# A linear-attention and feed-forward kernel: another written order of its steps, and GpSimd steps that wait for VectorE steps ahead of them

## The chip, the cores and the metric

The kernel runs on one core of a Trainium2 chip. A core has TensorE (PE, matrix products), VectorE (DVE), ScalarE (ACT), GpSimd (POOL) and SyncE (SP, which here issues all DMAs). Each engine works through its own queue in order; the queues are tied together by semaphores. The metric is the device time of one execution, in microseconds (us). A change is called faster or slower when it moves this time by more than 2%.

## The reference

Two parts follow each other. The first is a gated linear attention over 4 batches, 8 heads, 768 positions and a head width of 48; the second is a feed-forward part over the 3072 rows of 384 that come out.

```python
state = zeros((B, H, D, D))
for t in range(S):
    state = alpha[:, :, t, :, None] * state + einsum('bhd,bhe->bhde', k[:, :, t], v[:, :, t])
    y[:, :, t] = einsum('bhd,bhde->bhe', q[:, :, t], state)
x = y.transpose(0, 2, 1, 3).reshape(B * S, H * D)
h1 = x @ w1                      # 3072x384 @ 384x1024
h2 = x @ w2
out = maximum(h1, h2) @ w_out    # 1024x384
```

All inputs and the output are float32.

## The kernel before

**Tiling.** The 3072 positions are cut into twelve chunks of 256 (n = 0 to 11; three to a batch). A chunk needs four loads of 384 KB, alpha, k, q and v. For chunks 0 and 1 alpha is loaded in two halves, and many of the steps on them are cut in two as well, so `ka1.0` is the first half of step `ka` of chunk 1.

**A chunk's steps** (name, engine where it can go, line): `ln` the logarithm of alpha (ACT, L588); `su` the sum over pairs of positions (DVE or POOL, L596); `cs` the running sum by a triangular matrix (PE, L605 and L610); `inv`, `en`, `ep`, `gg` exponentials of it (ACT, L619 to L649); `ka` and `qi` products in place on k and q (DVE or POOL, L624, L629); `kt` and `qt` the scaled k and q in float16 (L661, L666); `vc` the cast of v (L488, L490 or L492, by engine); `tk` and `tq` their transposes (PE, L692), `ck` and `cq` the copies of these out of PSUM; from chunk 8 on DMA transposes `dk` and `dq` take the place of these four. `kv` makes the chunk's state terms (PE, L752); `t32`, `w` and `T` (L799, L810/L812, L787) carry the state on; `sc` the scores (PE, L832), `pt` their masked copy (DVE, L840); `yf` and `y` the output (PE, L877), and `xe` the cast of it into `xT` (ACT or DVE).

**The feed-forward part** uses max(h1, h2) = relu(x (w1 - w2)) + x w2. So `wd` forms w1 - w2 (L523), `wtp`/`wtc` transpose w2 (L507), `woc` casts w_out, and `mp`/`mc` form w2 times w_out (L532) once. The six weight loads are halves of w2, w_out and w1 (768 KB each; `ldw20`, `ldwo1` and so on, L467 and L470). Rows are worked in twelve groups of 256: `h` (PE, L943; `h0.4` is the product for the fifth and sixth of eight blocks of group 0), `r` the relu (L951 or L953), `o` the output product (PE, L976; parts a and b for each 128 rows), `ev` its copy out of PSUM, `st` the store. `h0.0` and `h0.2` need `wd0.0` and `wd0.1`; `h0.4` and `h0.6` need `wd1.0` and `wd1.1`.

**Fillers.** `fill` steps (L419) are products of a zero tile that nothing reads. They keep TensorE busy while it would wait in the opening.

**What sets the order.** Every step is declared to a planner with its dependencies, its possible engines and figures for its time (`plan.add`). The planner can search an order by itself, but where the text `ORDER` is not empty, `Plan.run` calls `Plan.follow` instead, which takes from that text the order of all steps, the engine of each (P, D, A, G, S) and the PSUM bank. The figures for time are then not read. The last loop of the kernel (L1007) emits the steps in that order. Dependencies between instructions on different engines become semaphore waits by what they read and write. `port=True` marks steps that the planner keeps from lying on VectorE and GpSimd at one time when it searches an order; before the change nothing in the emitted program enforces this.

SP's queue starts: `lda0.0 lda0.1 ldw21 lda1.0 ldk0.0 ldq0.0 lda1.1 ldw20 ldv0.0 ldwo0 ldw10 ldwo1 ldw11 ldq1.0 ldk1.0 ldv1.0`, then chunk 2.

Of the kernel before, what the change touches and what calls it, by code (L numbers as in the profile page):

```python
# [51 lines left out]
o0.1b:P inv2.0:A en2.0:A kt2.0:D y1:P xe3:D inv3.0:A ep2.0:A cs3.0:P5 tk2.0:P2 ev0.1:D xe2:A h1.0:P4 h1.2:P7 qi2.0:G qi3.0:G gg3.0:A en3.0:A ep3.0:A
r1.0:A h1.6:P1 ck2.0:D ka3.0:D kt3.0:G h1.4:P4 qt2.0:D r1.2:A gg2.0:A g2:G T4.1:G qt3.0:D vc2.0:A tq2.0:P o1.1a:P0 r1.4:A ldq4.0:S lda5.0:S r1.6:A
tk3.0:P6 ck3.0:A ln4.0:A inv4.0:A vc3.0:A kv2:P4 cq2.0:D sc2.0:P2 t32.4:G w4:D T4.0:G tq3.0:P T5.1:G pt2.0:D o1.1b:P o1.0a:P1 cq3.0:D ev1.1:D T5.0:G
yf2:P2 sc2.1:P4 pt2.1:D ldv4.0:S lda7.0:S sc3.1:P6 pt3.1:D su4.0:G cs4.0:P0 gg4.0:A en4.0:A ep4.0:A o1.0b:P ev1.0:A y2:P xe4:D xe5:A ka4.0:G qi4.0:G
qt4.0:D kt4.0:G ln5.0:A inv5.0:A kv3:P4 w6:D T7.0:G g4:G t32.7:G T7.1:G sc3.0:P6 pt3.0:D h2.0:P1 r2.0:A tk4.0:P2 ck4.0:A w7:D ldk5.0:S ldq5.0:S
h2.6:P0 tq4.0:P h2.4:P1 h2.2:P7 ldv5.0:S r2.6:D y3:P4 r2.2:D t32.8:G su5.0:D T8.0:D vc4.0:A kv4:P6 w8:D xe6:D cq4.0:A sc4.0:P2 r2.4:A xe7:A o2.0a:P0
t32.9:G qi5.0:G T9.1:G ln7.0:A inv7.0:A h3.0:P1 pt4.0:D o2.0b:P st0.0:S ev2.0:D lda6.0:S cs5.0:P5 gg5.0:A su7.0:D w9:D T8.1:G r3.0:A ka5.0:G en5.0:A
ln6.0:A ep5.0:A h3.2:P4 r3.2:D T9.0:D h3.6:P0 ldq6.0:S ldv6.0:S r3.6:A o2.1a:P1 h3.4:P4 r3.4:D ldk6.0:S yf4:P2 sc4.1:P6 pt4.1:D o2.1b:P ev2.1:A
qt5.0:D ldq7.0:S ldk7.0:S su6.0:G cs6.0:P4 gg6.0:A g5:G vc6.0:A en6.0:A ep6.0:A kt5.0:G ldv7.0:S lda8.0:S lda9.0:S o3.1a:P0 o3.0a:P1 cs7.0:P5 y4:P  # L60
ka6.0:D kt6.0:D kv6:P6 xe9:D w12:D T10.0:G inv6.0:A qi6.0:G t32.13:D w13:D o3.1b:P o3.0b:P ev3.1:D t32.10:G xe8:A ka7.0:G T10.1:G en7.0:A ep7.0:A
vc5.0:A gg7.0:A ev3.0:A h4.0:P3 tk5.0:P6 ck5.0:D r4.0:A qt6.0:D h4.2:P2 tq5.0:P cq5.0:D r4.2:A tk6.0:P0 ck6.0:A ldk8.0:S h4.4:P3 r4.4:A qi7.0:G
st0.1:S qt7.0:D ldk9.0:S lda10.0:S st1.1:S ldq9.0:S ldq8.0:S st1.0:S vc7.0:A tq6.0:P ln8.0:A cq6.0:A h4.6:P4 kv5:P6 sc5.0:P2 w10:D r4.6:D kt7.0:G
# [12 lines left out]
pt10.1:D st4.1:S st5.0:S o9.0a:P1 o9.1a:P0 vc11.0:A kv11:P6 t32.22:D w22:D T23.1:D T23.0:G y10:P xe20:A xe21:D sc11.0:P6 o9.1b:P ev9.1:A h10.0:P5
# [223 lines left out]
def kernel(  # L300
# [706 lines left out]
    for o in plan.run():  # L1007
        o.emit(o.eng)
# [31 lines left out]
```

## Time and profile before

| | us |
|---|---|
| median of 3 runs | 141.82 (141.81 to 143.49) |
| profiled execution | 141.61 |
| its span, first to last instruction | 139.8 |
| TensorE busy | 131.8 |
| VectorE busy | 100.2 |
| ScalarE busy | 80.5 |
| GpSimd busy | 67.7 |
| 41 fillers on TensorE | 13.3 |

HBM is read at 23.59 MB and written at 4.72 MB. The profile gives each engine's busy time in the span. Busy TensorE time contains fillers, and matrix products overlap the load of the next weights, so the time from the start of one step to the start of the next says more than the length of one instruction. Landing times of loads are read from the trace's DMA records: a load is in when the last of its sixteen pieces is. A line number, such as L943, is that of the kernel before.

### The profile page before, as it was taken

How to read it: one execution, taken by the hardware profiler on the slowest of the kernel's cores; microseconds unless marked ns; L12 is line 12 of the kernel's file. 1: busy time of each engine (PE TensorE's matmuls, PEld its weight loads, DVE VectorE, ACT ScalarE, POOL GpSimd, SP SyncE). 2: the span in 40 equal slices, each digit the busy share in tenths (PEclk: the TensorE clock that was granted, in tenths of full speed). 3: DMA queues.
4: the chain of work that ended last, by engine and by line, in shares of the span. 5: the costliest groups of instructions: out<-in, count | busy, mean ns of one | idle time of the engine just before them, and what ended most of it. 6: DMA issues, size and time to landing. Idle time of an engine off the chain costs nothing.

```text
span 139.8 us, 5453 instructions
## 1 busy us (share of the span) xinstructions
PE 131.8 (94%) x2346; PEld 93.7 (67%) x2346; DVE 100.2 (72%) x164; ACT 80.5 (58%) x163; POOL 67.7 (48%) x109
## 2 busy tenths in 40 slices
PE   6959996998999999999999999999999999999991
PEld 2336664754787687767886776777758866776770
DVE  7618657689997897797888959579876668583600
ACT  3337683677689599556897665674415552243041
POOL 6904390046858963885949996803850070300000
PEclk9999999999999999999999999999999999999999
DMA  4899999899999999999999999919904996545033
GB/s 110 268 277 329 355 382 333 201 251 267 266 253 266 262 267 282 248 232 235 274 272 266 312 279 122 250 26 208 288 24 77 187 202 182 177 155 188 4 109 113
DMA packets 64680, 30.76 MB, mean 220 GB/s; under 512 B 58896, under 2 KB 63120, under 8 KB 64656
## 3 DMA queue, kind: packets, MB, share of 16 engines
q1 hardware_dynamic: 64656, 30.41, 87.2%
q8 instruction: 18, 0.29, 0.9%
q14 instruction: 6, 0.05, 0.1%
HBM read 23.59 MB, written 4.72 MB: 202 GB/s over the span
## 4 chain that ended last, share of the span: by engine, by line
PE 73%; SPq 10%; DMA 9%; DVE 4%; issue 1%; ACT 1%; DVEq 0%
PE PS L976 31%; PE PS L943 21%; PE PS L877 9%; DMA ldf<-in_k_dram 9%; SPq L448 6%; PE PS L692 4%; PE PS L832 4%; SPq L467 3%; SPq L470 2%; PE PS L752 2%; PE PS L605 1%; DVE qk L490 1%; DVE w L812 1%; DVE ldf L629 0%; PE PS L419 0%
## 5 line engine op out<-in xcount | busy, mean ns | idle before, releaser
L976 PE MATMUL PS<-wo,g 128*128 128x384 f16 (+1 forms) x200 | 37.7, 320 | 0.0
L943 PE MATMUL PS<-xT,wd 128*128 128x256 f16 x288 | 35.9, 273 | 0.3 <-ACT xT L488 0.2
L840 DVE TENSOR_TENSOR pt<-PS,mask 128x1024 f16<-128x1024 f32 x24 | 28.9, 1218 | 6.1 <-PE PS L832 4.5
L943 PEld LDWEIGHTS <-wd 128*128 128x128 f16 x288 | 27.3, 98 | 5.4 <-DVE xT L490 0.6
L953 ACT ACTIVATE g<-PS 128x512 f16<-128x512 f32 x32 | 18.8, 598 | 13.0 <-PE PS L943 12.7
L976 PEld LDWEIGHTS <-g 128*128 128x128 f16 x200 | 18.6, 98 | 10.8
L488 ACT CAST xT<-PS 128x384 f16<-128x384 f32 x14 | 8.0, 592 | 17.2 <-PE PS L877 17.0
L787 POOL TENSOR_TENSOR T<-w,gg 48x192 f16<-48x192 f32 x17 | 9.4, 553 | 16.1 <-DVE w L812 9.8
L629 POOL TENSOR_TENSOR ldf<-ldf,inv 128x384 f32<-128x384 f32 (+1 forms) x10 | 9.8, 983 | 15.2 <-DMA ldf<-in_q_dram 13.3
L661 POOL TENSOR_TENSOR qkt<-ldf,en 128x768 f16<-128x768 f32 (+1 forms) x7 | 11.9, 1698 | 10.7 <-DVE ldf L624 8.5
L976 PE MATMUL PS<-m,xT 128*128 128x384 f16 (+1 forms) x75 | 15.8, 320 | 0.0
L419 PE MATMUL PS<-fz 128*128 128x512 f16 x41 | 13.3, 451 | 1.2 <-DVE fz L416 1.2
L588 ACT ACTIVATE loga<-ldf 128x768 f16<-128x768 f32 (+1 forms) x14 | 10.6, 754 | 5.7 <-DMA ldf<-in_alpha_dram 5.4
L951 DVE TENSOR_SCALAR g<-PS 128x512 f16<-128x512 f32 x16 | 10.9, 686 | 3.3 <-PE PS L943 3.2
L666 DVE TENSOR_TENSOR qkt<-ldf,PS 128x768 f16<-128x768 f32 (+1 forms) x14 | 11.6, 834 | 2.4 <-ACT PS L644 2.2
L692 PE MATMUL PS<-ident,qkt 128*128 128x128 f16 x128 | 10.3, 219 | 1.0 <-DVE qk L490 0.5
L488 ACT COPY outs<-PS 128x384 f32<-128x384 f32 (+1 forms) x15 | 6.8, 457 | 7.3 <-PE PS L976 6.4
L692 PEld LDWEIGHTS <-qkt 128*128 128x128 f16 x128 | 8.2, 97 | 3.5 <-issue 1.0
L877 PE MATMUL PS<-pt,v 64*64 64x128 f16 x576 | 10.2, 218 | 0.0
L596 POOL TENSOR_TENSOR s<-loga 128x384 f16<-128x384 f16 (+1 forms) x10 | 7.9, 799 | 4.4 <-ACT loga L588 4.2
L488 ACT COPY qk<-PS 128x1024 f16<-128x1024 f16 (+1 forms) x11 | 9.0, 820 | 1.8 <-PE PS L692 1.6
L488 ACT CAST v<-ldf 128x768 f16<-128x768 f32 (+1 forms) x11 | 8.1, 742 | 3.0 <-DMA ldf<-in_v_dram 3.0
(79 smaller groups left out, 199.3 us busy)
## 6 DMA issues: line engine op xcount, KB each, us to landing
ldf<-in_k_dram SPq DMA_DIRECT2D x12, 384.0 KB, 6.5
ldf<-in_q_dram SPq DMA_DIRECT2D x12, 384.0 KB, 5.8
ldf<-in_v_dram SPq DMA_DIRECT2D x12, 384.0 KB, 6.6
out_dram<-outs SPq DMA_DIRECT2D x23, 192.0 KB, 3.8
ldf<-in_alpha_dram SPq DMA_DIRECT2D x10, 384.0 KB, 5.8
ldf<-in_moe_w_dram SPq DMA_DIRECT2D x4, 768.0 KB, 8.1
ldf<-in_moe_w_out_dram SPq DMA_DIRECT2D x2, 768.0 KB, 9.8
ldf<-in_alpha_dram SPq DMA_DIRECT2D x4, 192.0 KB, 4.7
```

Source lines behind the costliest of these rows:

```text
L419: plan.add(f"fill{i}", {"PE": 0.21}, lambda eng: nc.tensor.matmul(bank(fb), lhsT=fz[:, 0:128], rhs=fz, start=True, stop=True, skip_group_c ...
L488: nc.scalar.copy(out=out, in_=in_)
L588: nc.scalar.activation(out=A["loga", n][:, hd].rearrange("p h j d -> p (h j d)"), in_=A["ld", n, "a"][:, hd].rearrange("p h d -> p (h d)") ...
L661: e.tensor_mul(out=hjd(qkts[i3], 1)[:, hd], in0=A["ld", n, "k"][:, hd].rearrange("p h (j d) -> p h j d", j=2), in1=f.unsqueeze(2).to_broad ...
L666: nc.vector.tensor_mul(out=hjd(qkts[i3], 0)[:, hd], in0=A["ld", n, "q"][:, hd].rearrange("p h (j d) -> p h j d", j=2), in1=f.unsqueeze(2). ...
L692: nc.tensor.transpose(t[:, a, r, j, :], src[:, j, r, :], ident16)
L840: nc.vector.tensor_mul(out=t.rearrange("p u r c -> p (u r) c"), in0=A["sc", n, hf].rearrange("p u (r c) -> p (u r) c", r=2), in1=mask.rear ...
L877: nc.tensor.matmul(dst, lhsT=lhsT, rhs=rhs, start=(x, u) not in begun, stop=done and ends[x, u] == i, skip_group_check=True)
L943: nc.tensor.matmul(t[:, i], lhsT=wd16[:, s, (f + i) * 128 : (f + i + 1) * 128], rhs=xT[:, s, a0 : a0 + W], start=(s == 0), stop=(s == 2), ...
L951: nc.vector.tensor_relu(o, i)
L953: nc.scalar.activation(out=o, in_=i, func=ACTF.Relu)
L976: nc.tensor.matmul(A["op", t0, c], lhsT=lhsT, rhs=rhs, start=(part == 0 and j == 0), stop=(part == 1 and j + 1 == len(todo[1])))
```

## The change

Three things are changed.

The text `ORDER` is replaced by another. It holds the same steps, with 43 fillers in place of 41. Both the order on each engine and the engine of some 100 steps differ. Among them: `pads0` goes to GpSimd, ahead of `setp1`; of `su`, `t32`, `qi`, `T`, `kt`, `ka` and `vc` 28 go from GpSimd to VectorE and 20 the other way; seven `vc` go from ScalarE to GpSimd. SP's queue now starts `lda0.0 ldw21 lda0.1 ldk0.0 ldq0.0 ldv0.0 ldw20 lda1.0 lda1.1 ldwo0 ldw10 ldwo1 ldw11 ldk1.0 ldq1.0 ldv1.0`. The order on the engines around chunk 1 and the first group:

```diff
 VectorE
-wd0.0 wd0.1 woc1.1 r0.0 wd1.0 wd1.1 qi1.1 ka1.0 kt1.0 ka1.1 qt1.1 ck1.0 qi1.0 qt1.0 w2 T3.1 cq1.0 su2.0 w3 pt1.0 pt1.1 kt2.0 xe3
+wd0.0 woc1.1 wd0.1 ka1.0 kt1.0 wd1.0 wd1.1 qi1.0 qt1.0 vc1.0 ck1.0 qt1.1 cq1.0 su2.0 w2 t32.3 ck1.1 w3 pt1.0 pt1.1 su3.0 kt2.0 xe2
 GpSimd
-T2.0 T2.1 kt1.1 t32.2 t32.3 T3.0 ka2.0 su3.0 qi2.0 qi3.0
+T2.1 T2.0 T1.1 t32.2 ka1.1 qi1.1 kt1.1 T3.1 T3.0 ka2.0 qi3.0 qi2.0
 TensorE
-mp0.1 mp0.2 mp0.0 fill h0.0 mp1.1 mp1.2 mp1.0 h0.2 h0.4 h0.6 o0.0a tk1.0 o0.0b kv1 tk1.1 tq1.0 fill tq1.1 fill fill fill sc1.0 o0.1a yf1 sc1.1 cs2.0 o0.1b y1
+mp0.0 mp0.2 mp0.1 h0.0 fill fill mp1.0 mp1.1 mp1.2 h0.2 tk1.0 h0.4 h0.6 o0.0a tq1.0 o0.0b kv1 tk1.1 fill tq1.1 sc1.0 o0.1a cs2.0 yf1 sc1.1 o0.1b y1
```

Some of the planner's figures are changed:

```diff
-xfer=(1.56 if n < 8 else 1.7) * (h1 - h0) / 8, lag=0.3 if n < 2 else 0.1))
+xfer=(1.535 if n < 8 else 1.63) * (h1 - h0) / 8, lag=0.5 if n == 1 and i else 0.35 if n < 3 else 0.15))
...
-    WX = {"w1": 786 / 370, "w2": 786 / 370, "wo": 2.12}
+    WX = {"w1": 2.12, "w2": 2.5, "wo": 2.12}
...
-xfer=WX[name], lag=1.3), buf)
+xfer=WX[name], lag={"w2": 2.0, "wo": 2.2, "w1": 2.8}[name]), buf)
...
-tr = plan.add(f"wtp{i}.{s}", {"PE": 0.74}, emit, ...
+tr = plan.add(f"wtp{i}.{s}", {"PE": 0.66}, emit, ...
```

And the loop that emits the steps makes the first instruction of a GpSimd step wait for the last VectorE step marked `port` that stands ahead of it in the order, unless an earlier GpSimd step already did. There are 25 such waits.

```diff
+    traced = nc.cur_bb.bb.instructions
+    ahead = None
     for o in plan.run():
+        n = len(traced)
         o.emit(o.eng)
+        if o.eng == "DVE" and o.port:
+            ahead = traced[-1]
+        elif o.eng == "POOL" and ahead is not None:
+            tc.add_manual_dep(traced[n], ahead.name,
+                              mybir.DependencyInfo(mybir.DependencyClass.Sync, mybir.DependencyReason.DATA), reason="port")
+            ahead = None
```

## The prediction

> **What bounds the kernel now.** I read the page first, then TensorE's busy time by stretches, then TensorE's and VectorE's timelines where the stretches show a loss, and last the pairs of VectorE and GpSimd instructions that lie beside each other. Part 1 of the page, two rows, and the engine row of the chain that ended last:
>
> ```profile
> PE 131.8 (94%) x2346; PEld 93.7 (67%) x2346; DVE 100.2 (72%) x164; ACT 80.5 (58%) x163; POOL 67.7 (48%) x109
> ...
> PE 73%; SPq 10%; DMA 9%; DVE 4%; issue 1%; ACT 1%; DVEq 0%
> ```
>
> TensorE is the engine that sets the end, but not from the start. The stretches (length, then busy time and instructions of PE, PEld, DVE, ACT, POOL, then granted clock, DMA share, GB/s) show where:
>
> ```profile
> 14.00:24.40 10.40, 9.26 (x168) 6.10 (x165) 6.69 (x10) 6.70 (x16) 4.49 (x9) 1.00 1.10 358
> 24.40:33.70 9.30, 8.55 (x97) 5.38 (x96) 7.62 (x15) 6.41 (x12) 3.38 (x5) 1.00 0.99 236
> 33.70:65.00 31.30, 31.11 (x640) 23.19 (x639) 27.43 (x40) 23.80 (x47) 21.57 (x30) 1.00 1.13 258
> 65.00:100.00 35.00, 34.87 (x750) 26.26 (x746) 27.87 (x43) 22.69 (x44) 23.95 (x31) 1.00 0.97 227
> 100.00:136.00 36.00, 35.87 (x637) 26.46 (x635) 22.46 (x34) 13.51 (x26) 7.11 (x11) 1.00 0.55 139
> ```
>
> From 33.7 to 136 us TensorE is idle 0.19 + 0.13 + 0.13 = 0.45 us: nothing that another engine does there can give much. What remains is the opening, where the chain runs over the loads, one of them the longest single piece (start, length):
>
> ```profile
> 15.57 12.70 DMA ldf<-in_k_dram
> ```
>
> That is chunk 1's k: landed at 28.27. TensorE's timeline from 24.4 us (start, length, line, operands, count, idle before and releaser):
>
> ```profile
> 24.42 2.11 PE L532 MATMUL PS<-wo,w2T 128*128 128x384 f16 x12 [1.07 <-ACT wo L488]
> 26.36 2.13 PE L943 MATMUL PS<-xT,wd 128*128 128x256 f16 x18
> 28.33 0.81 PE L976 MATMUL PS<-wo,g 128*128 128x384 f16 x4
> ...
> 31.85 0.38 PE L419 MATMUL PS<-fz 128*128 128x512 f16 x1
> 32.72 0.38 PE L692 MATMUL PS<-ident,qkt 128*128 128x128 f16 x4 [0.49 <-DVE qk L490]
> 32.94 0.81 PE L419 MATMUL PS<-fz 128*128 128x512 f16 x3
> 33.68 0.42 PE L832 MATMUL PS<-qk 48*64 48x128 f16 x16
> ```
>
> Starts from one step to the next give what a step costs: an `h` 0.66, `o…a` of an early group 0.65, `tk`/`tq` of a half chunk 0.22, a filler 0.21. Against that, this stretch loses 0.33 (after `o0.0a`, 0.98 long), 0.24 (after `tk1.1`), 0.87 (filler and wait before `tq1.1`) and three fillers, 0.65: 2.1 us. After 33.7 the same comparison finds about 1.2 us in all: 0.30 after `sc3.0`, 0.27 after `cs9.0`, 0.28 after `cs11.0`, the rest in pieces of 0.1. So 3.3 us is all that an order can win behind 24.4 us. Ahead of 24.42 it can win little: `mp1` needs `wo` half 1, which landed at 23.51, and its cast (0.83, to 24.37).
>
> **The figures in the plan (landing delays, transfer times, 0.66 for a transpose step).** They are read only where no order is written out; one is. Cost nothing.
>
> **The opening loads on SP's queue.** Same sixteen transfers in another order. Every prefix ends alike: through `wo` half 1 both orders hold the same twelve, so 23.5, and through `w1` half 1 the same thirteen (25.67). Chunk 0's v comes about 3.6 us earlier, chunk 1's alpha later (15.2 and 15.95 for its halves; they were 8.72 and 12.20), k of chunk 1 one place earlier (14th, where q landed at 26.89). Does alpha's delay reach `mp1`? ln1.0 15.75, su1.0 on GpSimd 16.35, t32.1 16.9, w1 on VectorE 17.35, T1.0 17.7, then pt0.1 and pt0.0 at 1.22 each: 20.15; y0 20.2 to 21.3 (before: 19.21 to 20.35), the xT cast and wd0.0 to 22.95, three `mp0` and `h0.0` to 23.95, two fillers to 24.4. It just fits: 0, without reserve. The setup moves on GpSimd (pads0 ahead of setp1, 1.3 us) delay the mask and su0.0 to about 6.7, where fourteen fillers of 0.43 cover it; the two fillers more (43 for 41) stand where TensorE waits for loads anyway: 0.
>
> **Chunk 1 on VectorE.** Before (start, length, idle before):
>
> ```profile
> 23.53 0.56 DVE L490 CAST wo<-ldf 128x768 f16<-128x768 f32 x1 [0.28 <-DMA ldf<-in_moe_w_out_dram]
> 24.01 0.68 DVE L951 TENSOR_SCALAR g<-PS 128x512 f16<-128x512 f32 x1
> 25.69 1.83 DVE L523 TENSOR_TENSOR wd<-ldf 128x768 f16<-128x768 f32 x2 [1.00 <-DMA ldf<-in_moe_w_dram]
> 27.44 0.35 DVE L629 TENSOR_TENSOR ldf<-ldf,inv 128x192 f32<-128x192 f32 x1
> 28.30 0.36 DVE L624 TENSOR_TENSOR ldf<-ldf 128x192 f32<-128x192 f32 x1 [0.51 <-DMA ldf<-in_k_dram]
> ```
>
> The wd pair begins the moment `w1` lands. In the new order ka1.0 and kt1.0 (0.36 + 0.56), which need k, stand ahead of wd1.0 and wd1.1 (0.95 each), which `h0.4` and `h0.6` need. k is queued behind `w1`, so VectorE now stands still for k with a ready wd behind it. With k at 26.89: ka1.0 27.3, kt1.0 27.9, wd1.0 28.85, wd1.1 29.75, qi1.0 30.1, qt1.0 30.65, vc1.0 31.0, ck1.0 31.4, qt1.1 31.95, cq1.0 32.4. TensorE: h0.2 to 27.03, tk1.0 28.2, h0.4 29.55, h0.6 30.45, o0.0a 31.1, tq1.0 31.35, o0.0b 32.5, kv1 32.85, tk1.1, one filler, tq1.1, and `sc1.0` at 33.55; before it was 33.68. Three fillers and their waits are gone, and about 2 us of new waiting before h0.4 has replaced them. When does k land? In the trace one of the sixteen pieces of `w1` half 0 landed 1.35 us behind the other fifteen (21.41 against 20.06), a 16 KB instruction fetch of 1.11 us lying on the DMA at 18.69, and that ring stays late down to q. Without it the 14th load is in at 25.66. Ends 25.66 and 26.89; I take the middle, 26.3, since a fetch hits some ring in either order, but not at a fixed place in it. `sc1.0` follows k: 32.95, so -0.7. Of this about 0.3 is given back: su3.0 (0.37, moved from GpSimd) now stands between pt1.1 and kt2.0 on VectorE, which has no idle from 34.4 to 37.7, and tk2.0 waits for kt2.0. Net -0.4; from the ends +0.1 and -1.1.
>
> **GpSimd's 25 waits.** A GpSimd step waits for the last of VectorE's steps marked as port users ahead of it in the order; all behind it in GpSimd's queue wait too. What it removes is seen here, first VectorE, then GpSimd:
>
> ```profile
> 58.16 1.09 DVE L596 TENSOR_TENSOR s<-loga 128x384 f16<-128x384 f16 x1
> ```
> ```profile
> 58.03 1.00 POOL L624 TENSOR_TENSOR ldf<-ldf 128x384 f32<-128x384 f32 x1
> ```
>
> A sum of 0.35 lasts 1.09 beside a GpSimd product. Added up over VectorE's su, t32, T and qi against the shortest of each form: 1.9 + 1.3 + 0.9 + 0.4 = 4.5 us, on GpSimd some 2.6. The Trainium skill ("SBUF — State Buffer", section "SBUF: two separate sides") says that the shared port pair is an exclusive lock and that the loser blocks for the whole instruction. That speaks against the wait: the hardware already lines the two up, so a semaphore can only choose who goes first, and for a copy with one input in SBUF (vc0.1, woc0.0, vc1.0, vc8.0: 4 of the 25 waits) outside the two-port modes it buys nothing. Taking the 4.5 us as won would give 137.1; by the lock rule it is a swap, gain 0. Mine is the trace's: TensorE idles 0.45 us after 33.7, so of the 4.5 only qi1.0's 0.38 at 30.24 lay on its path (inside the 2.1 above). The upper bound: ka1.1 now waits for qi1.0 (30.1), so qi1.1 and kt1.1 behind it end at 32.3 instead of 30.75, which kv1 needs; o0.0b covers that to 32.5. If h0.4 came without its wait the cover would go, and up to 1 us of it would show. I take 0, bounds -0.4 and +1.
>
> **Moved steps and SP's later queue.** With each moved step at its row's mean VectorE gets 0.8 us more, GpSimd loses 2.8, ACT 3: no bound changes. Chunk 3's v goes behind three loads of chunk 4: 46.3 instead of 42.04; its cast (0.82) is due before kv3 at 48.9, slack 1.8. Group 0's first store moves behind chunk 7's loads, landing about 67.4 instead of 56.2; the eighth output buffer is wanted at about 67.8: 0.4 to spare, then it would hold only a PSUM bank. Mode changes on TensorE: 54 in either order. pt5.1, which before ended 0.26 before y5, comes with some 9.95 us of VectorE work behind pt4.1 where 14.2 passed: slack instead. I count 0.7 of the 1.2 us of small losses as closed, bounds 0 and 1.1.
>
> **Sum and rivals.** The profiled execution took 141.61, 1.81 above its span of 139.8 and 0.2 below the median of 141.82. 141.6 - 0.4 - 0.7 = 140.5, and 0.1 for half of the distance to the median: 140.6.
> - Forecast, 140.6 (140.1 to 141.1), chance 0.50.
> - Swap: k at 26.89, the new wait for k eats the gap, and the late losses come back elsewhere: 141.5, chance 0.25. For it: k was 12.7 us under way. Against: fillers went.
> - All closed: k at 25.66, -1.1, and late losses -1.1: 139.4, chance 0.17. Against it: VectorE at 82% in that stretch and no slack at `mp1`.
> - Slower: VectorE's queue head. If k lands as late as before, 28.28, because a fetch hits its ring too, wd1.0 starts at 29.3, h0.4 at 30.3, and sc1.0 comes at 35.0: +1.3, 142.9, chance 0.08. It decides from a landing of about 27.0 on, one for one.
> - That the change does nothing of what it says: the figures do nothing; the lock already orders the engines. It then reduces to the swap.
>
> The range 139.2 to 142.2 leaves out most of the slower case and the lower third of "all closed". Within 2% (139.0 to 144.7, about what a measurement of this kernel can tell from no change) lies nearly all: faster 0.08 (half of "all closed"), slower 0.03.
>
> **What would show it.** VectorE idle some 1.3 us before L624 at 26 us, released by k's DMA; L943 after that released by VectorE's wd; one filler, not four, between 27 and 34; sc1.0 at about 33.0; no L596 on VectorE over 0.6; GpSimd waits with VectorE as releaser, and no PE wait on GpSimd. I am wrong if `mp1` starts after 24.6, if wd does not wait for k, or if TensorE idles over 1 us between 34 and 136.

## The result, and the profile after

| | before | after |
|---|---|---|
| median of the runs of the comparison (20 and 20) | 141.88 us | 141.22 us |
| profiled execution | 141.61 us | 140.77 us |
| its span | 139.8 us | 139.0 us |

The ratio is 0.9956, with a 95% interval of 0.9935 to 0.9976. Two later comparisons of the same kernel gave 0.9965 (0.9942 to 0.9987) and 0.9966 (0.9942 to 0.9989). The ratios leave out runs more than 1.5% above the fastest of their kernel, while the medians take in all. So the change gains 0.34 to 0.44%, or 0.5 to 0.6 us. The forecast of 140.6 stood for 1.2 us (141.82 to 140.6): the sign is right, the size is twice what came.

Part 1 of the page of after, two rows, and the engine row of the chain that ended last:

```profile
PE 132.2 (95%) x2348; PEld 93.8 (68%) x2348; DVE 96.2 (69%) x167; ACT 77.4 (56%) x160; POOL 63.9 (46%) x109
...
PE 74%; SPq 9%; DMA 9%; ACT 2%; DVE 2%; issue 1%; DVEq 0%; ACTq 0%
```

The bound is the same: TensorE, behind an opening that hangs on loads. VectorE is busy 4.0 us less although it has three instructions more. The prediction's count of the moved steps alone gave it 0.8 us more, so the 4.5 us that it lost beside GpSimd are about gone. The time shows a small part of them. The stretches of after (length, then busy time and instructions of PE, PEld, DVE, ACT, POOL, then granted clock, DMA share, GB/s):

```profile
14.00:24.40 10.40, 10.38 (x176) 6.91 (x175) 7.30 (x12) 7.01 (x17) 3.75 (x8) 1.00 1.09 356
24.40:33.70 9.30, 8.01 (x106) 5.23 (x105) 6.87 (x16) 6.09 (x12) 2.87 (x5) 1.00 1.07 245
33.70:65.00 31.30, 30.82 (x623) 22.88 (x622) 26.33 (x42) 22.93 (x46) 19.76 (x25) 1.00 1.14 269
65.00:100.00 35.00, 35.00 (x751) 26.60 (x750) 28.07 (x43) 21.84 (x43) 23.23 (x36) 1.00 1.02 219
100.00:136.00 36.00, 35.90 (x638) 26.48 (x635) 19.14 (x29) 13.51 (x29) 7.18 (x13) 1.00 0.53 131
```

TensorE's idle time from 33.7 to 136 us is 0.48 + 0 + 0.10 = 0.58 us; before it was 0.45. Nothing was won there by this count. Between 24.4 and 33.7 it even idles 1.29 us, where it idled 0.75. The chain of after still holds chunk 1's k, which is in at 26.02 (before at 28.27):

```profile
13.96 12.06 DMA ldf<-in_k_dram
```

VectorE's timeline of after, around that landing (start, length, idle before and its releaser at the end):

```profile
23.03 0.95 DVE L523 TENSOR_TENSOR wd<-ldf 128x768 f16<-128x768 f32 x1
26.05 0.36 DVE L624 TENSOR_TENSOR ldf<-ldf 128x192 f32<-128x192 f32 x1 [2.07 <-DMA ldf<-in_k_dram]
26.52 0.56 DVE L661 TENSOR_TENSOR qkt<-ldf,en 128x384 f16<-128x384 f32 x1
26.99 1.82 DVE L523 TENSOR_TENSOR wd<-ldf 128x768 f16<-128x768 f32 x2
```

And TensorE's timeline of after in the same stretch:

```profile
23.59 2.11 PE L532 MATMUL PS<-wo,w2T 128*128 128x384 f16 x12
25.54 0.82 PE L943 MATMUL PS<-xT,wd 128*128 128x256 f16 x6
27.13 0.40 PE L692 MATMUL PS<-ident,qkt 128*128 128x128 f16 x4 [0.77 <-DVE qkt L661]
28.00 1.70 PE L943 MATMUL PS<-xT,wd 128*128 128x256 f16 x12 [0.47 <-DVE wd L523]
...
32.24 0.38 PE L419 MATMUL PS<-fz 128*128 128x512 f16 x1
...
32.77 0.42 PE L832 MATMUL PS<-qk 48*64 48x128 f16 x16
```

This is the picture that was foreseen: VectorE stands 2.07 us for k with the two `wd` ready behind it, TensorE waits for `tk1.0` and for `h0.4`, one filler is left, and `sc1.0` starts at 32.77. The new waits of GpSimd are there too; two rows of what GpSimd waited for in after (us in total, times, longest):

```profile
POOL T L787 <- DVE qkt L661: 2.6, 1, 2.6
POOL ident L407 <- DVE s L596: 2.5, 1, 2.5
```

The first is `T21.0` behind `kt11.0`, the second `id32` behind `su0.1`.

The pair of profiled executions cannot say where the 0.6 us came from. Their spans differ by 0.8 us, and `mp1` starts 0.83 us earlier in after (23.59 for 24.42), so behind `mp1` both take 115.4 us. A second profiled execution of the unchanged kernel has `mp1` at 23.49, so 0.83 us is no more than the loads spread by from one execution to the next. The experiments below use medians of many runs for what a change is worth, and traces for where.

### The profile page after: what moved, and what is told of

Same layout as the page of the kernel before. It is cut to its first block, busy times and chain, and to the rows that moved or that the text cites. A ratio compares the mean times of both kernels' runs of the same rounds, so it can differ in the third digit from the quotient of the medians.

```text
span 139.0 us, 5466 instructions
## 1 busy us (share of the span) xinstructions
PE 132.2 (95%) x2348; PEld 93.8 (68%) x2348; DVE 96.2 (69%) x167; ACT 77.4 (56%) x160; POOL 63.9 (46%) x109
## 3 DMA queue, kind: packets, MB, share of 16 engines
HBM read 23.59 MB, written 4.72 MB: 204 GB/s over the span
## 4 chain that ended last, share of the span: by engine, by line
PE 74%; SPq 9%; DMA 9%; ACT 2%; DVE 2%; issue 1%; DVEq 0%; ACTq 0%
PE PS L976 31%; PE PS L943 22%; PE PS L877 9%; DMA ldf<-in_k_dram 9%; SPq L448 5%; PE PS L692 5%; PE PS L832 4%; SPq L470 3%; PE PS L752 2%; SPq L467 2%; PE PS L605 1%; DVE pt L840 1%; ACT xT L488 1%; DVE wd L523 1%; ACT loga L588 1%
## 5 line engine op out<-in xcount | busy, mean ns | idle before, releaser
L943 PE MATMUL PS<-xT,wd 128*128 128x256 f16 x288 | 36.4, 273 | 0.8 <-DVE wd L523 0.5
L787 POOL TENSOR_TENSOR T<-w,gg 48x192 f16<-48x192 f32 x19 | 10.1, 534 | 17.1 <-DVE w L812 3.7
L419 PE MATMUL PS<-fz 128*128 128x512 f16 x43 | 14.3, 453 | 1.2 <-DVE fz L416 1.2
L951 DVE TENSOR_SCALAR g<-PS 128x512 f16<-128x512 f32 x15 | 10.1, 686 | 6.5 <-PE PS L943 4.5
L624 POOL TENSOR_TENSOR ldf<-ldf 128x384 f32<-128x384 f32 (+1 forms) x9 | 8.3, 924 | 11.1 <-DMA ldf<-in_alpha_dram 9.1
L488 ACT COPY outs<-PS 128x384 f32<-128x384 f32 (+1 forms) x19 | 8.5, 464 | 6.7 <-PE PS L976 6.4
L787 POOL TENSOR_TENSOR T<-w,g 48x192 f16<-48x192 f32 x14 | 7.1, 509 | 7.5 <-PE PS L877 3.9
L661 POOL TENSOR_TENSOR qkt<-ldf,en 128x768 f16<-128x768 f32 (+1 forms) x6 | 10.1, 1678 | 0.0
L877 PEld LDWEIGHTS <-v 64*64 64x64 f16 x576 | 8.6, 107 | 2.2 <-issue 1.7
L832 PE MATMUL PS<-qk 48*64 48x128 f16 x384 | 9.6, 219 | 0.1
```

Of the source, the lines that this page charges most:

```text
L419: plan.add(f"fill{i}", {"PE": 0.21}, lambda eng: nc.tensor.matmul(bank(fb), lhsT=fz[:, 0:128], rhs=fz, start=True, stop=True, skip_group_c ...
L488: nc.scalar.copy(out=out, in_=in_)
L787: e.tensor_mul(out=T16s[m % 4][o : o + 48, :, 48 * u : 48 * u + 48], in0=w_[o : o + 48], in1=g_[o : o + 48])
L832: nc.tensor.matmul(t[64 * x : 64 * x + 64, u, c0 : c0 + 128].rearrange("p (j m) -> p j m", j=2), lhsT=qk[o : o + D, 1, j, r, 64 * x : 64 * ...
L877: nc.tensor.matmul(dst, lhsT=lhsT, rhs=rhs, start=(x, u) not in begun, stop=done and ends[x, u] == i, skip_group_check=True)
L943: nc.tensor.matmul(t[:, i], lhsT=wd16[:, s, (f + i) * 128 : (f + i + 1) * 128], rhs=xT[:, s, a0 : a0 + W], start=(s == 0), stop=(s == 2), ...
```

## The experiments

### Order and waits apart

Four kernels make a square: old or new order, without or with the new loop.

**after_again** is the changed kernel once more, no edit.

> The changed kernel once more, so that its variants are compared with it on one chip. Known: 0.9956 of before. Theory Opening (the gain is the earlier work between 23.6 and 33 us): sc1.0 within 0.4 us of 32.8 and mp1 at 23.6 again, if the earlier landing of w_out half 1 (22.5 against 23.5) comes with the order. Rival Chance: mp1 starts anywhere from 23.5 to 24.5 from run to run, and the 0.8 us by which it was earlier is not the order's.

**after_nowait** keeps the new order and takes the loop back:

```diff
-    traced = nc.cur_bb.bb.instructions
-    ahead = None
     for o in plan.run():
-        n = len(traced)
         o.emit(o.eng)
-        if o.eng == "DVE" and o.port:
-            ahead = traced[-1]
-        elif o.eng == "POOL" and ahead is not None:
-            tc.add_manual_dep(...)
-            ahead = None
```

> The changed kernel without the 25 waits of GpSimd, its order kept. Theory Swap (the hardware lines the two engines up anyway, TensorE does not wait for either): within 0.2% of the changed kernel, and long VectorE sums and products (over 0.6 us) come back. Rival Wait-pays: the waits are what gained; the time goes back by 0.6 us or more, to that of before.

**before_wait** is the other corner: the old order with the new loop, which makes 24 waits there.

```diff
+    traced = nc.cur_bb.bb.instructions
+    ahead = None
     for o in plan.run():
+        n = len(traced)
         o.emit(o.eng)
+        if o.eng == "DVE" and o.port:
+            ahead = traced[-1]
+        elif o.eng == "POOL" and ahead is not None:
+            tc.add_manual_dep(...)
+            ahead = None
```

> The kernel before with GpSimd waiting for VectorE by the new rule, its old order kept. The changed kernel without its waits was 1.66% slower than the kernel before, so the waits are worth 2% in the new order. Theory Place (a collision costs only where its VectorE step stands on TensorE's path; in the old order only qi1.0 does, 0.38 us): within 0.4% of the kernel before. Rival Everywhere (the 4.5 us that VectorE loses in the old order are worth as much as in the new one): 1 to 2% faster.

**after_third** and **before_wait_2** are the changed kernel and the kernel of before_wait again, side by side on one chip.

> The changed kernel once more, beside the old order with the new rule. Theory Waits (all of the gain is the waits; the new order with them is worth what the old one is): 0.996 of the kernel before, and within 0.3 us of the next run, either side. Theory Order (the order's opening and closed stalls are worth something on top, as the forecast had it): at least 0.4 us below the next run.

> The old order with the new wait rule, on the chip of the run above. Theory Waits: 0.996 of the kernel before, equal to the changed kernel within 0.3 us. Theory Order: 0.4 us or more above the changed kernel.

Measured, as ratios to the kernel before in the same comparison, with 95% intervals:

| | without waits | with waits |
|---|---|---|
| old order | 1 | 0.9958 (0.9933 to 0.9982), again 0.9986 (0.9960 to 1.0012) |
| new order | 1.0166 (1.0114 to 1.0219), 144.73 us | 0.9956, 0.9965, 0.9966 (intervals above) |

The new order alone makes the kernel 1.7% slower, by about 2.4 us, which neither of the two expectations had. Of its six runs four enter the ratio, and all six (143.50 us and more) lie above the slowest of the 49 runs of the kernel before beside them (143.28). With the waits the new order is 0.4% faster. So in the new order the waits are worth 2.0%.

In the old order they are worth 0 to 0.4%: in the second comparison the median of all 22 runs, 141.45 us, is not below the 141.19 of the kernel before. What the new order adds to the old one with the same waits is little. Side by side on one chip it is 0.2% by the ratios, whose intervals overlap, and 0.4% by the medians of all runs (140.86 and 141.45); across the first comparisons it is 0 (0.9956 and 0.9965 against 0.9958).

### One wait in the new order

In the trace of after_nowait the VectorE products that stand long beside GpSimd are `kt9.0` (3.02 us; 0.95 alone), `kt2.0` (1.76; 0.95), `su4.0` (1.52; 0.35), `qi5.0` (1.25; 0.55), `qi1.0` (1.15; 0.35), `vc0.1` (1.22; 0.35) and `wd1.1` (1.34; 0.95). The largest was taken for a test of its own.

**no_t14_wait** is the changed kernel without one wait of the 25, that of `T14.0` for `kt9.0`:

```diff
         elif o.eng == "POOL" and ahead is not None:
-            tc.add_manual_dep(...)
+            if o.name != "T14.0": tc.add_manual_dep(...)
```

> The changed kernel with 24 of its 25 waits: that of T14.0 behind kt9.0 is left out. Theory Train (a VectorE product that meets GpSimd's queue full of work is kept off the port through several GpSimd instructions, not one): kt9.0 lasts about 3 us instead of 0.95, TensorE waits over 1 us before y6, and the time is 1.0 to 1.7 us above the changed kernel. Rival One-for-one (the loser waits for one instruction): kt9.0 under 2 us and no more than 0.3 us on the time.

Measured: 142.24 us, 1.0057 (1.0034 to 1.0081): 0.9 to 1.0% above the changed kernel, some 1.3 us for one wait. VectorE's timeline of no_t14_wait, then GpSimd's, then TensorE's:

```profile
81.31 3.02 DVE L661 TENSOR_TENSOR qkt<-ldf,en 128x768 f16<-128x768 f32 x1
84.25 2.34 DVE L840 TENSOR_TENSOR pt<-PS,mask 128x1024 f16<-128x1024 f32 x2
```
```profile
81.09 0.50 POOL L787 TENSOR_TENSOR T<-w,g 48x192 f16<-48x192 f32 x1
81.56 1.00 POOL L629 TENSOR_TENSOR ldf<-ldf,inv 128x384 f32<-128x384 f32 x1
82.52 0.99 POOL L624 TENSOR_TENSOR ldf<-ldf 128x384 f32<-128x384 f32 x1
```
```profile
83.21 0.82 PE L943 MATMUL PS<-xT,wd 128*128 128x256 f16 x6
85.51 0.41 PE L877 MATMUL PS<-qk,T 112*64 112x128 f16 x8 [1.49 <-DVE pt L840]
```

`kt9.0` starts while `T14.0` runs, and waits for it, for `qi8.0` and for `ka8.0`: 83.51 is the end of the third, 0.82 us before the end of `kt9.0`. GpSimd's three lose nothing (0.50, 1.00, 0.99 are their lengths alone). Behind `kt9.0` on VectorE stands `pt6.1`, for which TensorE then waits 1.49 us. The same place in after_again, VectorE and GpSimd:

```profile
81.60 0.95 DVE L661 TENSOR_TENSOR qkt<-ldf,en 128x768 f16<-128x768 f32 x1
```
```profile
82.63 0.50 POOL L787 TENSOR_TENSOR T<-w,g 48x192 f16<-48x192 f32 x1 [1.32 <-ACT en L640]
```

`T14.0` starts 1.03 us after the start of `kt9.0`, where in no_t14_wait it started 0.22 us ahead of it, and nobody waits for it. (The row names a step of ScalarE that ends at the same moment; `T14.0` reads nothing of it. It starts 0.08 us after `kt9.0` ends, at 82.55.)

**early_waits** keeps only the first seven waits, those up to `T3.1`:

```diff
         elif o.eng == "POOL" and ahead is not None:
-            tc.add_manual_dep(...)
+            if o.name in ("id32", "vc0.0", "g1", "t32.2", "ka1.1", "kt1.1", "T3.1"): tc.add_manual_dep(...)
```

> The changed kernel with the first seven waits alone (id32, vc0.0, g1, t32.2, ka1.1, kt1.1, T3.1). Without any it lost 2.9 us to the changed kernel. Theory Place: the opening's waits save 0.7 to 1.2 us of that, the later ones (T14.0's alone 1.3) the rest, so this one is 1.7 to 2.2 us above the changed kernel, and kt2.0, su4.0 and kt9.0 are long again. Rival Opening: the opening's waits are nearly all of it, within 0.5 us of the changed kernel.

Measured: 142.56 us, 1.0081 (1.0043 to 1.0119), about 1.2% or 1.7 us above the changed kernel. The trace has `kt9.0` at 3.00 us again, and TensorE waits 1.47 us at the same place; 0.66 us more go within `y8`, in a pause with no semaphore behind it. So of the 2.0% some 1.2% hang on waits behind `T3.1`, most of it on the one at `kt9.0`. The rest hangs on the first seven waits, and the largest piece that after_nowait shows there is `vc0.1`. VectorE's timeline of after_nowait, then of after:

```profile
12.83 1.22 DVE L490 CAST v<-ldf 128x384 f16<-128x384 f32 x1
```
```profile
11.68 0.35 DVE L490 CAST v<-ldf 128x384 f16<-128x384 f32 x1
```

With `vc0.1`, `w0` behind it is late, `t32.1` waits for `w0`, and `mp1` starts 9.41 us after the second half of chunk 1's alpha is in. In after it starts 8.53 us after it, so 0.88 us are lost there. The collisions of `kt2.0` and `su4.0` cost TensorE 0.70 us (at `tk2.0`) and 0.67 us (at `sc3.1`) in after_nowait. In early_waits `kt2.0` is back at 0.95 us and `su4.0` at 0.56, although their own waits are left out: they hang on what came before. The expectation had them long again. These are losses of single executions; the ratios are not split further.

**no_copy_waits** drops the four waits behind VectorE copies of one input (`vc0.1`, `woc0.0`, `vc1.0`, `vc8.0`):

```diff
+            if o.name not in ("vc0.0", "t32.2", "kt1.1", "qi9.0"): tc.add_manual_dep(...)
```

> The changed kernel without the four waits on a VectorE copy with one input in SBUF (vc0.0, t32.2, kt1.1, qi9.0). The prediction said that they buy nothing. Theory Cast-is-held (the probe's cast took 1.03 us beside products and 1.52 beside memsets, alone 0.34): vc0.1 lasts about 1.2 us beside pads1, y0 and with it mp1 come 0.5 to 0.9 us later, and the time is 0.3 to 0.9 us above the changed kernel. Rival Nothing: within 0.2 us.

Measured: 141.07 us, 0.9982 (0.9958 to 1.0006), beside a kernel before of 141.26; the changed kernel had no run in that comparison, and of its three ratios elsewhere two lie inside this interval and one 0.0002 below it. Not told apart. The copies do lose time: `vc0.1` lasts 0.66 us for 0.35, `vc8.0` 0.93 for 0.56. Neither shows on TensorE: `w0` behind `vc0.1` ends at 15.40 us, before GpSimd is done with `su1.0` (15.44), which stands ahead of `t32.1` in its queue; and from `kv2` to the end that trace takes 96.6 us, no more than the changed kernel.

### One wait in the old order

`kt9.0` has a counterpart in the old order. VectorE's timeline of before, then GpSimd's:

```profile
77.36 1.17 DVE L799 TENSOR_TENSOR t<-w,gg 112x192 f32<-112x192 f32 x1
78.66 0.36 DVE L812 TENSOR_TENSOR w<-PS,t 112x192 f32<-112x192 f32 x1
```
```profile
77.30 1.01 POOL L624 TENSOR_TENSOR ldf<-ldf 128x384 f32<-128x384 f32 x1
```

`t32.15` lasts 1.17 us beside `ka9.0`; `w15` behind it reads the PSUM pair into which `tk7.0` writes next, and TensorE loses 0.27 us between `cs9.0` and `tk7.0`. TensorE's timeline of before, the end of `cs9.0` and `tk7.0`:

```profile
78.70 0.24 PE L610 MATMUL PS<-gcol,s 128*128 128x4 f16 x4
79.07 0.61 PE L692 MATMUL PS<-ident,qkt 128*128 128x128 f16 x8
```

**before_one_wait** is before_wait with one of its 24 waits, which puts `su8.0`, and with it `ka9.0`, behind `t32.15`:

```diff
-            tc.add_manual_dep(...)
+            if o.name == "su8.0": tc.add_manual_dep(...)
```

> The old order with one of the rule's 24 waits, GpSimd's su8.0 behind VectorE's t32.15. In the kernel before t32.15 lasts 1.17 us instead of 0.36 beside GpSimd's ka9.0, and the cast w15 behind it frees the PSUM pair for which tk7.0 on TensorE waits 0.26 us. Theory One place: this wait is most of what the rule is worth in the old order: t32.15 0.36 us, no wait ahead of tk7.0, 0.3 us below the kernel before (0.9975) and at most 0.3 us above the run with all 24. Theory Many places: 0.1 us or less below the kernel before, t32.15's wait gone or not.

Measured: 140.79 us, 0.9961 (0.9934 to 0.9988), with a span of 138.5 us. VectorE's timeline of before_one_wait, then TensorE's:

```profile
76.38 0.36 DVE L799 TENSOR_TENSOR t<-w,gg 112x192 f32<-112x192 f32 x1
76.87 0.36 DVE L812 TENSOR_TENSOR w<-PS,t 112x192 f32<-112x192 f32 x1
```
```profile
77.72 0.24 PE L610 MATMUL PS<-gcol,s 128*128 128x4 f16 x4
77.83 0.61 PE L692 MATMUL PS<-ident,qkt 128*128 128x128 f16 x8
```

`t32.15` takes 0.36 us, `tk7.0` follows `cs9.0` after its 0.28 us without a wait, and from `y4` to `y6` TensorE needs 19.59 us where the two executions of before needed 19.94 and 19.93. These 0.35 us lie inside the interval of the ratio (0.17 to 0.93 us). One wait is worth what all 24 are worth, within what these runs can tell; and one wait in the old order is worth what the whole change is.

### Who gets the port

Three kernels leave the kernel's work out and run VectorE steps beside trains of GpSimd steps.

**port_probe** has plain 128x384 products, casts and memsets. The rows of a trial:

```python
for i in range(m):
    nc.gpsimd.tensor_mul(out=ts[i], in0=gate, in1=c)   # or a copy and memsets
nc.vector.tensor_copy(out=s, in_=PS[:, 0:384])
nc.vector.tensor_mul(out=r, in0=a, in1=b)              # or a cast of a, or of PS
```

> No attention and no feed-forward part, zeros go out: one VectorE instruction on 128x384 is started while GpSimd works through 1, 2, 4 or 8 products of about 1.0 us that wait for nothing, or through memsets. Theory Train: the VectorE product (0.55 alone) ends behind the last GpSimd product, so it lasts about 0.5, 1.5, 3.5 and 7.5 us. Rival One-for-one: never over 1.6 us. A copy out of PSUM is not held by anything; whether a cast with one SBUF input is held by products or by memsets is open.

VectorE's product lasts 0.54 us alone and 1.16, 1.15, 1.16, 1.16 beside trains of 1, 2, 4 and 8 GpSimd products: it loses to one and comes before the next. The casts, in VectorE's timeline of port_probe: alone, beside four products, beside a copy and three memsets, and at the end a cast out of PSUM beside four products:

```profile
25.91 0.34 DVE L53 CAST h<-a 128x384 f16<-128x384 f32 x1
...
26.99 1.03 DVE L53 CAST h<-a 128x384 f16<-128x384 f32 x1
...
31.62 1.52 DVE L53 CAST h<-a 128x384 f16<-128x384 f32 x1
...
35.32 0.54 DVE L55 CAST h<-PS 128x384 f16<-128x384 f32 x1
```

A cast of float32 out of SBUF with one input is held like a product. It runs at a higher rate than the one out of PSUM (0.34 for 0.54 us), which is the sign of a mode with both ports: the Trainium skill ("VectorE: DVE Perf Modes", section "Mode 2×_2P — use both read ports for one tensor") says that single-source steps out of SBUF can use both read ports and that a source in PSUM cannot; the rows agree on both.

**port_probe2** takes the kernel's own shapes (`kt`, `su`, `t32`) against trains of one kind, `ka` or `T`:

```python
nc.gpsimd.tensor_mul(out=ks[i][:, :, 0:48], in0=ks[i][:, :, 0:48], in1=gate[:, :, 48:96])   # ka, m times
nc.vector.tensor_copy(out=s, in_=PS[:, 0:384])
nc.vector.tensor_mul(out=q16..., in0=a..., in1=b...)                                        # kt
```

> No attention and no feed-forward part, zeros go out: VectorE's kt, su and t32 in their own shapes, and a product of 128x384, each started while GpSimd works through 1 or 4 products in the shape of ka or of T. In the first probe a VectorE product lost to one GpSimd product only, in the kernel kt9.0 lost to three in a row. Theory Shape (what is written in float16, or read through a broadcast, is kept off through the whole queue): kt and su last over 3 us beside four ka, the float32 product 1.2. Rival One-for-one: none over 2 us, and the three in a row have another cause.

`kt` lasts 0.94 us alone, 1.56 beside one `ka`, 1.55 beside four and 1.07 beside four `T`; `su` and `t32` last 0.34 alone and 1.03 beside four `ka`. One product lost in every trial, so this does not yet make the kernel's 3.02.

**port_probe3** takes short trains of the kernel's own mix:

```python
TRIALS = (("kt", "TqkgG"), ("kt", "TkkG"), ("kt", "TqG"), ("kt", "kqkG"), ("kt", "gkkG"),
          ("su", "TkG"), ("su", "TkkG"), ("kt", "ktTkG"), ("kt", "TTkkG"))
```

(`q` is `qi`, `k` is `ka`, `t` is `t32`; `G` closes a trial with a small step.)

> The kernel's work is left out; VectorE runs kt's product (0.94 us alone) or su's sum (0.34 us alone) beside short trains of GpSimd products: T, qi, ka, g in the kernel's own order and shapes (T 48 partitions x 192, qi and ka 128 x 384, g 112 x 4), then T, ka, ka; T, qi; ka, qi, ka; g, ka, ka; the sum beside T, ka and T, ka, ka; and two more. Theory Kind (a short 48-partition product ahead of full ones makes VectorE lose to all of them): kt's product about 3.0 us beside T, qi, ka and the sum 1.5 us beside T, ka, as in the kernel, and about 1.55 us beside ka, qi, ka. Theory Elsewhere (something else of the full kernel is needed): at most one GpSimd product lost in every trial, 1.0 to 1.6 us for kt's product and 0.4 to 1.1 us for the sum.

Two of its trials, `T q k g` and `k q k`, VectorE's timeline first and then GpSimd's:

```profile
10.91 2.97 DVE L63 TENSOR_TENSOR q<-a,b 128x768 f16<-128x768 f32 x1
...
23.83 1.35 DVE L63 TENSOR_TENSOR q<-a,b 128x768 f16<-128x768 f32 x1
```
```profile
10.66 0.50 POOL L50 TENSOR_TENSOR T<-w,g 48x192 f16<-48x192 f32 x1 [10.22 <-DVE w L47]
11.12 0.98 POOL L54 TENSOR_TENSOR qx<-qx,inv 128x384 f32<-128x384 f32 x1
12.07 0.99 POOL L56 TENSOR_TENSOR k<-k,gate 128x384 f32<-128x384 f32 x1
13.03 0.92 POOL L58 TENSOR_TENSOR gp<-w,gg 112x4 f32<-112x4 f32 x1
...
23.37 0.99 POOL L56 TENSOR_TENSOR k<-k,gate 128x384 f32<-128x384 f32 x1 [1.00 <-DVE gate L46]
24.32 1.71 POOL L54 TENSOR_TENSOR qx<-qx,inv 128x384 f32<-128x384 f32 x1
```

The first trial is the kernel's case in all its numbers: 2.97 us for `kt`, three GpSimd products in a row at their own speed, and the fourth step (0.92 for 0.20) held in its turn. In the second, VectorE loses only to the first product, and the next one on GpSimd (1.71 for 0.98) waits for VectorE. All trials, from the trace:

| VectorE step | GpSimd train | its length, us (alone) | GpSimd products it lost to |
|---|---|---|---|
| kt | T q k g | 2.97 (0.94) | 3 |
| kt | T k k | 2.97 | 3 |
| kt | T q | 2.02 | 2 |
| kt | g k k (starts in the first k) | 2.66 | 2 |
| kt | T T k k | 3.50 | 4 |
| kt | k q k | 1.35 | 1 |
| kt | k t T k | 1.35 | 1 |
| su | T k | 1.42 (0.34) | 2 |
| su | T k k | 2.43 | 3 |

In these trials, trains that begin with a short product keep VectorE off until their last full product is done, and the small step behind it then waits for VectorE; trains that begin with a full one let it in after the first. Why is not settled: the train of four `T` in port_probe2, whose source was strided and not contiguous, lost one only.

### The opening and the late losses

**before_again** is the kernel before, unchanged, one profiled execution.

> The kernel before, one more profiled execution. Theory Opening: w_out half 1 lands at 23.5 again and mp1 starts near 24.4. Rival Chance: w2 half 1 lands anywhere from 6.3 to 8 us and mp1 starts 0.5 us or more off 24.4; then the 0.8 us between the two profiles at mp1 says nothing of the order.

**wd_first** is the changed kernel with the new wait for k taken off `wd1.0` and `wd1.1`:

```diff
 VectorE
-wd0.1 ka1.0 kt1.0 wd1.0 wd1.1 qi1.0
+wd0.1 wd1.0 wd1.1 ka1.0 kt1.0 qi1.0
 TensorE
-h0.2 tk1.0 h0.4 h0.6 o0.0a
+h0.2 h0.4 h0.6 tk1.0 o0.0a
```

> The changed kernel with wd1.0 and wd1.1 put back ahead of ka1.0 and kt1.0 on VectorE, and tk1.0 behind h0.6 on TensorE. Theory Queue head (VectorE standing still for k with a ready wd behind it costs TensorE 1.7 us before o0.0a): h0.6 ends near 27.6 instead of 29.5, sc1.0 near 31.5 instead of 32.8, and the time is 0.6 to 1.2 us below the changed kernel. Rival Supply: what follows is bound by VectorE's chain and the loads of chunk 2; the gain is taken back by y1, and the time is within 0.3 us of the changed kernel.

**k_first** loads chunk 1's k one place earlier, ahead of w1's second half:

```diff
 SP
-ldw10 ldwo1 ldw11 ldk1.0 ldq1.0
+ldw10 ldwo1 ldk1.0 ldw11 ldq1.0
```

> The changed kernel with chunk 1's k loaded ahead of w1 half 1. k lands near 24.2 and w1 half 1 near 26.0. Theory Queue head: ka1.0 starts near 24.3, wd1.0 at 26.0, h0.4 at 27.1 and h0.6 at 28.0 instead of 28.9; 0.5 to 0.9 us below the changed kernel. Rival Supply: within 0.3 us of it.

**wd_first_o7** is wd_first with `o7.0b` moved behind `cs11.0`, so that the cast of `y8` has time before `h9.0`:

```diff
 TensorE
-o7.1b o7.0b y9 y8 kv10 cs11.0 h9.0
+o7.1b y9 y8 kv10 cs11.0 o7.0b h9.0
```

> The changed kernel with wd1.0 and wd1.1 ahead of ka1.0 and kt1.0 on VectorE, tk1.0 behind h0.6, and o7.0b moved behind cs11.0 on TensorE, so that the cast of y8 is done when h9.0 comes. Theory: 0.3 us for the first part (that is what wd_first kept), 0.25 for the wait before h9.0 that all traces show: 0.992 to 0.994 of before. Rival Supply: both are given back, 0.996.

Measured: wd_first 141.11 us, 0.9940 (0.9910 to 0.9969); k_first 141.37 us, 0.9954 (0.9934 to 0.9974); the changed kernel beside them 0.9965 (0.9942 to 0.9987). wd_first_o7 140.96 us, 0.9978 (0.9955 to 1.0002), in another comparison. before_again took 141.45 us. No variant is told apart from the changed kernel, and none beats it beyond its interval. The starts of TensorE's steps in the traces say why (us; the last column is the span less the start of `kv2`):

| | mp1 starts | mp1 to sc1.0 | sc1.0 to kv2 | mp1 to kv2 | kv2 to end |
|---|---|---|---|---|---|
| before | 24.42 | 9.26 | 9.16 | 18.42 | 96.96 |
| before_again | 23.49 | 9.41 | 9.28 | 18.69 | 97.52 |
| before_wait | 23.40 | 9.90 | 9.16 | 19.06 | 96.54 |
| before_wait_2 | 24.87 | 9.41 | 9.16 | 18.57 | 97.36 |
| before_one_wait | 23.30 | 9.42 | 9.16 | 18.58 | 96.62 |
| after | 23.59 | 9.18 | 9.42 | 18.60 | 96.81 |
| after_again | 23.36 | 9.29 | 9.72 | 19.01 | 96.73 |
| after_third | 23.60 | 8.95 | 9.88 | 18.83 | 96.97 |
| k_first | 24.12 | 7.73 | 10.35 | 18.08 | 97.00 |
| wd_first | 24.80 | 7.57 | 10.62 | 18.19 | 96.91 |
| wd_first_o7 | 23.47 | 8.02 | 10.22 | 18.24 | 97.79 |
| after_nowait | 25.41 | 8.56 | 10.04 | 18.60 | 99.39 |

Three things are to be read here. First, most of what comes earlier at `sc1.0` is later given back: from `mp1` to `sc1.0` wd_first and k_first take 1.2 to 1.7 us less, and by `kv2` 0.4 to 0.9 are left. The rest goes behind `cs2.0`, `cs3.0` and `h1.6`, where TensorE waits for steps that stand behind the loads of chunks 2 and 3. In wd_first these are `T3.0`, behind `su2.0`, which waits for chunk 2's alpha, and `kt2.0`, for which ScalarE first waits for chunk 3's alpha. The loads land at a pace of one in 1.3 to 2.4 us. In wd_first and k_first `mp1` starts 0.5 to 1.4 us later than in the changed kernel, which shortens any wait for a load behind it, and might be all that is left. But wd_first_o7, with `mp1` at 23.47, is at `kv2` 0.4 to 0.8 us sooner too. Whether a part is kept stays open; the ratios do not show it.

Second, the new order has another load ahead of `mp1`. In the eight traces that keep the opening's waits, `mp1` starts 8.52 to 8.54 us after the second half of chunk 1's alpha is in. In four of the five traces of the old order it starts 0.91 us after w_out half 1 is in. Most of the spread of `mp1` is that of these loads.

Third, behind `kv2` the old order takes 96.96 and 97.52 us, with all its waits 96.54 and 97.36, with one wait 96.62; the changed kernel takes 96.73 to 96.97, and the new order without waits 99.39. Only the last stands apart.

In wd_first_o7 the wait between `cs11.0` and `h9.0` (0.25 us in after_again) is gone, but a pause of 0.48 us at `y8` with no semaphore behind it stands two steps earlier in that execution, so its gain isn't seen.

## Why the prediction was right in sign and wrong in size

**The planner's figures, `mp1`, the moved setup.** Taken at nothing, and no change of `mp1` beyond the spread came: it starts at 23.36 to 23.60 us in three executions of the changed kernel, against 23.49 and 24.42 before. The walk from alpha to `mp1` was right, and so was its "without reserve": it took 8.45 us from the landing of alpha's second half (15.95 to 24.4), and 8.53 were measured. Alpha was in 0.9 us sooner (15.06). What the walk did not say is that it holds only with the waits; without them it is 9.41. The figures were not tried alone, and nothing reads them.

**Chunk 1 on VectorE, -0.4.** The mechanism is as foreseen: VectorE idle for k (2.07 us, foreseen some 1.3), k in at 26.02 (26.3), one filler, `sc1.0` at 32.77 (33.0). That k came so near is in part luck: 26.3 was the middle of a case with a late piece and one without, and in after one piece is late again (by 1.23 us) in a queue that runs some 0.9 us sooner. The step that failed is "of this about 0.3 is given back". By `kv2` all of it is: from `mp1` on, before took 18.42 and 18.69 us, after 18.60 to 19.01. The term measures about 0 or a little above, not -0.4. The walk stopped at `sc1.0`; the next loads set the pace up to `kv2`.

**GpSimd's 25 waits, 0.** This is the step that failed in kind. "So of the 4.5 only qi1.0's 0.38 lay on its path" counted TensorE's idle time in the old order. Two things were missed. One lay in the trace of before: the 0.27 us after `cs9.0` was listed as a late loss, but not followed to `w15` and `t32.15`, whose 1.17 us belong to those very 4.5; one wait there gives 0.9961. The other could not be read off the old trace: the waits stand in the new order, and that order without them takes 1.7% more. A term of the change has to be priced in the program that the change makes.

**The lock rule and the swap.** "A semaphore can only choose who goes first": the rule, an exclusive lock for a whole instruction, agrees with the rows, but the conclusion drawn from it does not. VectorE loses not one turn but up to four (0.94 to 3.50 us in port_probe3), the places are not equal, since `pt6.1` and TensorE wait behind VectorE's product and nobody behind GpSimd's, and so the choice is worth 1.3 us at `kt9.0`. The trace of before had a sign of it, VectorE first and then GpSimd:

```profile
32.70 1.52 DVE L596 TENSOR_TENSOR s<-loga 128x384 f16<-128x384 f16 x1
```
```profile
32.55 0.50 POOL L787 TENSOR_TENSOR T<-w,gg 48x192 f16<-48x192 f32 x1
33.02 0.99 POOL L624 TENSOR_TENSOR ldf<-ldf 128x384 f32<-128x384 f32 x1
```

A sum of 0.35 us that loses to a `T` and to the `ka` behind it. The prediction showed only the case with one product. That the four waits behind one-input copies buy nothing stands unrefuted in time (no_copy_waits), but its reason was wrong: those casts are held.

**Late losses, -0.7.** This step failed as well. The same sums over after give some 1.2 us again. `cs9.0`'s is gone. The ones after `sc3.0` (0.30) and `cs11.0` (0.25) stand, because the steps around them (`y2 kv3 sc3.0 h2.0` and `y8 kv10 cs11.0 h9.0`) are the same in both orders, which the text of the order shows. New ones came after `o0.1b` (0.33, for `pt1.1`) and at `sc4.0` (0.29, no semaphore). The term is about 0.

**The sum.** -0.4, 0 and -0.7 were forecast. Measured, the new order is worth between 0 and -0.6 us with its waits, where the traces find neither of the two terms that were to give it, and +2.4 us without them; the waits are worth -2.8 us in it. So the two terms that carried the forecast came to about nothing, and the one put at 0 is the one without which the change is a loss. That the sign came out right is luck as far as the argument goes: three terms were mis-sized, and their errors mostly cancel. The end, 141.22, lies between the forecast and the swap (141.5); the swap's reason, a lock that orders the engines anyway, is refuted by after_nowait. The slower case (k's landing) did not come. No rival had the mechanism that decides here: an order that lives by its waits. Of what "would show it", all came in after: `sc1.0` and the filler, VectorE's wait for k, GpSimd's waits, no sum on VectorE over 0.6 us (in after_again one of 0.74), no TensorE wait on GpSimd, and 0.58 us of idle TensorE between 33.7 and 136. None of its signs of being wrong came. A trace can show every step of a forecast and not its price.

**What stays open.** The changed kernel's own 0.6 us is not placed event by event: behind `kv2` its three executions are 0.3 to 0.5 us shorter than the average of the two of before (97.24), and ahead of `mp1` the loads spread by 0.9 us in the same kernel. The spread behind `kv2` in one kernel is as large (96.54 and 97.36 in the old order with its waits). Whether the new order adds 0 or up to 0.4% to the old one with waits is below what these runs resolve. Nor is it known why some trains of GpSimd steps keep VectorE off to their end.

## What to carry to other kernels

Where VectorE and GpSimd share work, look for VectorE steps that last two or three times their shortest, and follow each to the TensorE step behind it; a single semaphore at that place may give all that a rule for every place gives. Price a new order and a new wait together and in the new program: collisions move with the order. And carry a gain in an opening on to the point where the next loads bind, not to the first step that comes early.

## What the runs showed of the hardware

- VectorE can lose the shared port to up to four GpSimd products in a row (0.94 to 3.50 us), while GpSimd loses nothing meanwhile; with other trains it loses to one. What decides is open.
- A float32 to float16 cast out of SBUF is held like a two-input product: 0.34 us alone, 1.03 beside products, 1.52 beside a copy and three memsets. The same cast out of PSUM is not (0.54 and 0.54).
- In the trace of before, one of the sixteen pieces of a load (w1 half 0) landed 1.35 us behind the rest, with a 16 KB instruction fetch of 1.11 us just before (18.69 us), and the three loads behind it have a late piece too. In before_again, with such a fetch at 18.78, no piece of that load is late by more than 0.18. The load behind it, w_out half 1, is in at 23.51 and at 22.58, and `mp1` starts at 24.42 and 23.49. That the fetch is what delays the piece is argued from the times and was not tried.
